# A fused attention and gated-FFN kernel: sums of x and weight sums move to other places and to another engine

## The chip, the cores and the metric

The kernel runs on one core of one Trainium2 chip. The metric is the time of one execution on the device in microseconds (us). The core has a matrix engine (TensorE; in the profile PE, and PEld for its weight loads), a vector engine (VectorE, DVE), a scalar engine (ScalarE, ACT), GpSimd (POOL), a queue engine that issues transfers here (SyncE, SP), and DMA engines that carry the transfers. Matmul results are written to PSUM, which is held here as four tiles of two banks each; everything else on the chip lies in SBUF.

## The reference, cut to what matters

A sigmoid attention of 8 sequences of 448 with 12 heads of 64 is followed by a gated feed-forward block on the 3584 x 768 result.

```python
def _attn_ref(q, k, v):                      # (8, 12, 448, 64) each
    scores = scale * np.matmul(q, k.transpose(0, 1, 3, 2)) - np.log(S)
    attn = 1.0 / (1.0 + np.exp(-scores))
    return np.matmul(attn, v)

def _moe_ref(x, w_gate, w_val, w_out):       # x (3584, 768), w_gate and w_val (768, 1536), w_out (1536, 768)
    g = x @ w_gate
    silu = g * (1.0 / (1.0 + np.exp(-g)))
    val = x @ w_val
    return silu * val @ w_out
```

## The kernel before

The 8 sequences are taken in four pairs (pb = 0 to 3). A quad is four heads of one sequence, so there are 24 quads, n = 0 to 23, three to a sequence (NJ = 3), and quad n belongs to sequence n // 3. Each quad has 7 attention tiles (C = 7). The attention of later sequences is laid between the feed-forward work of earlier ones as "visits" of three or four attention tiles.

For the first three pairs the first stage is ffn1 (12 units of 12 matmuls for each sequence) and the output stage is ffn2 and ffn2_group. The groups use Strassen-like sums: 7 block products in place of 8, for which sums of the hidden values h (make_sums, on VectorE) and of the output weights (w_sum, on VectorE) are needed. The last pair (FAST) does its first stage in the same way, in six steps of `double`: it needs sums of x (x_sums) and of the gate and value weights (fast_w).

The sums of the gate and value weights. There are 4 slices of them (s = 0 to 3). Slices 0 and 1 are made on GpSimd in pieces of 384 columns, three to a sum; slices 2 and 3 on VectorE in one piece each. The sums of kind 1 are written over the weights themselves:

```python
    def fast_w(s, kind, i=None):
    ... (b11, b12, b21, b22 are blocks of the gate and value weights, t is the output)
        a, b, op = {
            3: (b22, b12, SUB), 1: (b12, b11, SUB), 2: (b22, gT.get((s, 1), gT[(s, kind)])[:, js], SUB),
            4: (b21, gT.get((s, 2), gT[(s, kind)])[:, js], SUB),
        }[kind]
        (V if i is None else G).tensor_tensor(out=t, in0=a, in1=b, op=op)
```

The sums of x. They are formed when the last of the two sequences' quads of one index has left PSUM, so for quads 21, 22 and 23 (j = 0, 1, 2). The third is written over one of its operands:

```python
    def x_sums(pb, j):

        a11, a12 = xT[(2 * pb, 2 * j)], xT[(2 * pb, 2 * j + 1)]
        a21, a22 = xT[(2 * pb + 1, 2 * j)], xT[(2 * pb + 1, 2 * j + 1)]
        if j == 0:
            ts = [half_of(ramp_a)[:, 8 * FW * hw + i * S:8 * FW * hw + (i + 1) * S] for i in range(3)]
        else:
            ts = [xtp.tile([128, S], FP16, tag="xT", name=f"xS{i}_{pb}_{j}") for i in range(3)]
        s1, s2, s4 = ts
        V.tensor_tensor(out=s1, in0=a21, in1=a22, op=ADD)
        V.tensor_tensor(out=s2, in0=s1, in1=a11, op=SUB)
        V.tensor_tensor(out=a21, in0=a11, in1=a21, op=SUB)
        V.tensor_tensor(out=s4, in0=a12, in1=s2, op=SUB)
        xS[(pb, j)] = (s1, s2, a21, s4)
```

They are called at the end of pv, the product of attention and v, behind the casts that bring its result from PSUM to x:

```python
    ...
        x = xtp.tile([128, S], FP16, tag="xT", name=f"xT_{b}_{2 * j}")
        first = nc.vector.tensor_copy(out=x, in_=P[:, 0, :S])
        xT[(b, 2 * j)] = x
        x = xtp.tile([128, S], FP16, tag="xT", name=f"xT_{b}_{2 * j + 1}")
        xT[(b, 2 * j + 1)] = x
        halves = [(x[w * 64:(w + 1) * 64, :], P[(1 - w) * 64:(2 - w) * 64, 1, :S]) for w in range(2)]
        done = [nc.vector.tensor_copy(out=o, in_=i) for o, i in halves[how:]]
        if how == 2:
            for o, i in halves:
                apart(nc.scalar.copy(out=o, in_=i), first)
        sums = lambda: x_sums(b // 2, j) if b // 2 in FAST and b % 2 else None
        if how != 1:
            sums()

        def rest():
            if how == 1:
                o, i = halves[0]
                apart(nc.scalar.copy(out=o, in_=i), first, *done)
                sums()

        return rest
```

A double step uses the products in the order 1, 2, 6, 5, 7, 3, 4, each for two hidden blocks f; product 6 is the first that reads sums of x and of weights:

```python
        prods = {
            1: (w(wg16, 0), x(b0, 0)), 2: (w(wg16, 1), x(b0, 1)), 3: (w(wv16, 1), xs(4)), 4: (ws(4), x(b1, 1)),
            5: (ws(1), xs(1)), 6: (ws(2), xs(2)), 7: (ws(3), xs(3)),
        }
```

A group of the output stage. TensorE may write bank 0 again (product 6) when VectorE has taken product 1 out of it:

```python
        o1 = osp.tile([128, DM], FP32, tag="osb", name="osb")
        mm(1, 0, True, False)
        snap(0, o1, 0)
        mm(2, 1, True, True)
        put(1, o1, 0)
        ...
        mm(6, 0, False, False)
        snap(0, o1, 1)
        ... (products 5, 7, 3, 4 in the same way)
```

The order of the output stage's units, with the eight output weight sums of the first pair:

```python
        o_units = [(0.0, make_sums, (99,)), (FU2, ffn2, (pb, C - 1))]
        if pb == 0:

            ts = [(0.0, w_sum, (s, kind)) for s in range(2) for kind in (3, 2, 1, 4)]
            o_units += ts[:4] + [(FU2, ffn2, (pb, 0))] + ts[4:] + [(FU2, ffn2, (pb, 3))]
        for g in range(1 if pb == 0 else 0, 3):
            o_units.append((FU3, ffn2_group, (pb, g)))
        units += o_units
```

The attention's transfers. `fetch` issues the loads of a quad from GpSimd, `casts` turns q and k to bf16 on GpSimd, `trans` issues their DMA transposes from SyncE, and `hold` keeps GpSimd's queue until the transposes have landed, so that the loads behind it don't start sooner:

```python
    def fetch(n):
        load(n, 0, G)
        load(n, 1, G)
        load_v(n)
...
    def casts(n):
        cast(n, 0, G)
        cast(n, 1, G)

    def trans(n):
        trans_dma(n, 0)
        trans_dma(n, 1)

    def ready(n):
        casts(n)
        trans(n)

    held = one.tile([128, 2], BF16, tag="held", name="held")

    def hold(n):
        for w in range(2):
            G.tensor_copy(out=held[:, w:w + 1], in_=qT[(n, w, C - 1)][:, :1])
...
    plan = {
        (3, 2): ((casts, 5), (post.append, 4)),
        (3, 4): ((post.append, 5),),
        (4, 0): ((fetch, 6),),
        (4, 4): ((ready, 6),),
        (5, 4): ((hold, 6), (fetch, 7), (w_out, 0)),
        (6, 0): ((ready, 7),),
        (6, 4): ((hold, 7), (fetch, 8), (w_out, 1)),
        (7, 0): ((ready, 8),),
        (7, 4): ((hold, 8), (fetch, 9), (w_out, 2), (w_out, 3)),
        (8, 0): ((ready, 9),),
        (8, 4): ((hold, 9), (fetch, 10), (casts, 10)),
        (9, 0): ((trans, 10), (fetch, 11)),
    }
    for n in range(9, NQ):
        if n + 2 < NQ:
            plan[(n, 4)] = ((casts, n + 2),)
            plan[(n + 1, 0)] = ((trans, n + 2),)
        if n + 3 < NQ:
            plan[(n, 4)] += ((fetch, n + 3),)
```

A key (n, c) is done in the visit that holds attention tile c of quad n.

The loop that emits everything; its last lines place the weight sums of slices 0 and 1:

```python
    for at, (fn, args, how) in enumerate(seq):
        if fn is None:
            pvs, pend = pend, []
            attn_step(args, pvs, how)
            ... (the plan's actions)
        if pend and (... or fn is double or how):
            for n in pend:
                pv(n)
            pend = []
        fn(*args)
        if fn is ffn1 and args[0] == 2 * (B // 2 - 1) - 1 and args[1] == NF - 1:
            for sl in range(2):
                for kind in (3, 1, 2, 4):
                    for i in range(JT):
                        fast_w(sl, kind, i)
```

The order of emission around the third pair's output stage, as this code gives it: ffn1 of sequence 5 with the visits of quads 20 to 22; make_sums; ffn2(2, 6); visit of quad 23 with pv(22); ffn2_group(2, 0); visit of quad 23's last tiles; ffn2_group(2, 1); pv(23); ffn2_group(2, 2); the six double steps of the last pair. At quads 8 to 10, in the output stage of the first pair: visit (8, 0); two units of ffn1; visit (8, 4); ffn2(0, 6); four output weight sums; ffn2(0, 0); visit (9, 0) with pv(8); four output weight sums; ffn2(0, 3); visit (9, 4); ffn2_group(0, 1); visit (10, 0) with pv(9).

Of the kernel before, what the change touches and what calls it, by code (L numbers as in the profile page):

```python
# [14 lines left out]
ADD = mybir.AluOpType.add  # L15
SUB = mybir.AluOpType.subtract
# [4 lines left out]
def kernel(  # L21
# [13 lines left out]
    B, H, S, D = q.shape  # L35
    DM = H * D
    DFF = moe_w_gate.shape[1]
    C = S // D
    NJ = H // 4
    NP = H // 2  # L40
    NF = DFF // 128
# [101 lines left out]
    def half_of(a):  # L143
        return a.rearrange("p a b s -> p (a b s)").bitcast(FP16)
# [76 lines left out]
    def trans_pe(n):  # L221
        D2 = Banked()
        ds = [qkT.tile([128, C, 128], BF16, tag=f"T{w}", name=f"T{w}_{n}") for w in range(2)]
        for f in [trans_part(D2, w, n, w, 0, C, nc.vector, ds[w]) for w in range(2)]:
            f()
        qT[(n, 0)] = ds[0]
# [34 lines left out]
    def pv(n, how=0, at=None):  # L261
# [25 lines left out]
# [6 lines that stand above are left out]
# [10 lines left out]
    V, G = nc.vector, nc.gpsimd  # L303
# [44 lines left out]
    HF = NF // 2  # L348
    JT = NP // 2
# [3 lines left out]
    def fast_w(s, kind, i=None):  # L353

        js = slice(0, JT) if i is None else slice(i, i + 1)
        b11, b21 = wg16[s][:, 0::2][:, js], wg16[s][:, 1::2][:, js]
        b12, b22 = wv16[s][:, 0::2][:, js], wv16[s][:, 1::2][:, js]
        if (s, kind) not in gT:
            if kind == 1:
                gT[(s, 1)] = wv16[s][:, 0::2]  # L360
            else:
                at = s * 3 + (3, 2, 4).index(kind)
                a = half_of(stg_a) if at < 6 else pt_a.rearrange("p a b s -> p (a b s)")
                n = JT * FW * 128
                gT[(s, kind)] = a[:, at % 6 * n:(at % 6 + 1) * n].rearrange("p (j n) -> p j n", j=JT)
        t = gT[(s, kind)][:, js]
# [3 lines that stand above are left out]
        }[kind]  # L370
        (V if i is None else G).tensor_tensor(out=t, in0=a, in1=b, op=op)

    xS = {}

    def x_sums(pb, j):
# [5 lines that stand above are left out]
        else:  # L381
            ts = [xtp.tile([128, S], FP16, tag="xT", name=f"xS{i}_{pb}_{j}") for i in range(3)]
        s1, s2, s4 = ts
        V.tensor_tensor(out=s1, in0=a21, in1=a22, op=ADD)
        V.tensor_tensor(out=s2, in0=s1, in1=a11, op=SUB)
        V.tensor_tensor(out=a21, in0=a11, in1=a21, op=SUB)
        V.tensor_tensor(out=s4, in0=a12, in1=s2, op=SUB)
        xS[(pb, j)] = (s1, s2, a21, s4)

    def double(pb, fs, extra=()):  # L390
# [68 lines left out]
    hS = {}  # L459
# [161 lines left out]
    FU1, FU2, FU3, FU4 = 2.26, 3.9, 6.83, 7.85  # L621
# [3 lines left out]
    for pb in range(B // 2):  # L625
        if pb in FAST:
            late = [(s, kind) for s in (2, 3) for kind in (3, 1, 2, 4)]
            for f in range(0, NF, 2):
                extra = [lambda a=a: fast_w(*a) for a in (late[f:f + 2] if f < 8 else [])]
                units.append((FU4, double, (pb, (f, f + 1), extra)))  # L630
                tt += FU4
        for b in (2 * pb, 2 * pb + 1) if pb not in FAST else ():
            f1_start[b] = tt
            for f in range(NF):
                if b or f > 2:
                    units.append((FU1, ffn1, (b, f)))
                tt += FU1
            f1_end[b] = tt
        o_units = [(0.0, make_sums, (99,)), (FU2, ffn2, (pb, C - 1))]
        if pb == 0:  # L640

            ts = [(0.0, w_sum, (s, kind)) for s in range(2) for kind in (3, 2, 1, 4)]
            o_units += ts[:4] + [(FU2, ffn2, (pb, 0))] + ts[4:] + [(FU2, ffn2, (pb, 3))]
        for g in range(1 if pb == 0 else 0, 3):
            o_units.append((FU3, ffn2_group, (pb, g)))
        units += o_units
        tt += sum(u[0] for u in o_units)
# [8 lines left out]
    for grp in visits:  # L656
        n, c = grp[0]
        b, j = divmod(n, NJ)
# [6 lines left out]
    def attn_step(group, pvs, how):  # L665
        for part in (group[:2], group[2:]):
            scs = [(n, c, qk_tile(n, c)) for n, c in part]
            rest = [pv(pvs.pop(0), how) for _ in range(len(pvs))]
            for i, (n, c, sc) in enumerate(scs):

                sig_tile(n, c, sc, split=len(group) == 4 and part[0] == group[0] and i == 1)
            for f in rest:
                f()
# [50 lines left out]
    held = one.tile([128, 2], BF16, tag="held", name="held")  # L724
# [70 lines left out]
    for f, Df in enumerate(early):  # L795
# [14 lines left out]
        (6, 4): ((hold, 7), (fetch, 8), (w_out, 1)),  # L810
        (7, 0): ((ready, 8),),
        (7, 4): ((hold, 8), (fetch, 9), (w_out, 2), (w_out, 3)),
        (8, 0): ((ready, 9),),
        (8, 4): ((hold, 9), (fetch, 10), (casts, 10)),
        (9, 0): ((trans, 10), (fetch, 11)),
    }
    for n in range(9, NQ):
# [31 lines left out]
# [4 lines that stand above are left out]
            if at == last_visit:  # L853
                nc.scalar.preload_act_table(SILU)
            for n, c in args:
                for act, of in plan.get((n, c), ()):
                    act(of)
                if c == C - 1:
                    pend.append(n)
            while post:  # L860
                trans_pe(post.pop())
            continue
        if pend and (fn is ffn1 and args[1] == 0 and (args[0], NP - 1) not in xT or fn is double or how):
            for n in pend:
                pv(n)
            pend = []
        fn(*args)
        if fn is ffn1 and args[0] == 2 * (B // 2 - 1) - 1 and args[1] == NF - 1:
            for sl in range(2):
                for kind in (3, 1, 2, 4):  # L870
                    for i in range(JT):
                        fast_w(sl, kind, i)


# [28 lines left out]
```

## Time and profile before

| what | value |
|---|---|
| time, median of 3 executions | 414.78 us (414.24 to 425.22) |
| profiled execution, span from first to last instruction | 412.3 us |
| mean granted TensorE clock | 0.994 of full speed |
| busy: TensorE matmuls, VectorE, ScalarE, GpSimd | 96%, 65%, 52%, 29% of the span |
| 24 weight sums on GpSimd, 128 x 384 each | 22.3 us busy |
| sums of x on VectorE, 12 of 128 x 448 | 4.7 us busy |
| sums of h on VectorE, 96 of 128 x 384 | 39.1 us busy |

How to read the profile. Times are counted from the span's start. L311 is line 311 of the kernel. A line of the timeline gives the start, the duration, the engine, the line, the operation, output and inputs by the program's names with their shapes, how many, and in brackets the idle time before it with what ended it. A line of the list of waits says which instruction waited for which, with the total, the number and the longest. The chain of waits is followed back from the last instruction, at each step to what released it; its pieces have a start, a length and what it was. A busy TensorE need not be at its peak, because the ends of its pipelined matmuls are modelled.

### The profile page before, as it was taken

How to read it: one execution, taken by the hardware profiler on the slowest of the kernel's cores; microseconds unless marked ns; L12 is line 12 of the kernel's file. 1: busy time of each engine (PE TensorE's matmuls, PEld its weight loads, DVE VectorE, ACT ScalarE, POOL GpSimd, SP SyncE). 2: the span in 40 equal slices, each digit the busy share in tenths (PEclk: the TensorE clock that was granted, in tenths of full speed). 3: DMA queues.
4: the chain of work that ended last, by engine and by line, in shares of the span. 5: the costliest groups of instructions: out<-in, count | busy, mean ns of one | idle time of the engine just before them, and what ended most of it. 6: DMA issues, size and time to landing. Idle time of an engine off the chain costs nothing.

```text
span 412.3 us, 7991 instructions
## 1 busy us (share of the span) xinstructions
PE 397.2 (96%) x3158; PEld 206.3 (50%) x3158; DVE 269.6 (65%) x503; ACT 216.3 (52%) x332; POOL 119.1 (29%) x156
## 2 busy tenths in 40 slices
PE   7799999999989999999999999998998899999995
PEld 3445444545555454444555545444554455555563
DVE  3737565877944655587655556569966667996753
ACT  5966877554434666557454365755653226657100
POOL 4628051452535255330030333439400000000000
PEclk8999999999999999999999999999999999999999
DMA  8999968978899999751068797820002420000135
GB/s 267 248 255 244 228 135 127 199 162 155 249 202 320 171 193 191 194 131 13 13 129 232 181 164 134 148 45 2 1 2 67 126 78 1 2 1 0 40 81 148
DMA packets 59844, 54.38 MB, mean 132 GB/s; under 512 B 35744, under 2 KB 53280, under 8 KB 59808
## 3 DMA queue, kind: packets, MB, share of 16 engines
q0 software_dynamic: 18880, 30.94, 35.1%
q1 hardware_dynamic: 40496, 22.62, 26.5%
q8 instruction: 24, 0.39, 0.4%
q10 hardware_dynamic: 432, 0.33, 0.3%
q14 instruction: 12, 0.10, 0.1%
HBM read 47.19 MB, written 11.01 MB: 141 GB/s over the span
## 4 chain that ended last, share of the span: by engine, by line
PE 76%; DMA 15%; DVE 6%; POOL 1%; issue 1%; SPq 0%; ACT 0%; DVEq 0%; POOLq 0%
PE ps_D L311 32%; PE ps_D L542 16%; PE ps_D L409 12%; DMA T<-c 8%; PE ps_D L272 7%; PE ps_D L239 6%; PE ps_D L600 3%; DMA stg_a<-in_k_dram 2%; DMA v<-in_v_dram 2%; DMA stg_a<-in_q_dram 2%; DVE S L501 1%; DVE xT L286 1%; POOL c L190 1%; DMA st<-in_q_dram 1%; DVE xT L281 1%
## 5 line engine op out<-in xcount | busy, mean ns | idle before, releaser
L258 ACT ACTIVATE pt_a<-ps_D 128x896 f16<-128x896 f32 x148 | 127.2, 919 | 76.5 <-PE ps_D L239 74.1
L311 PE MATMUL ps_D<-xT,wg 128*128 128x448 f16 x432 | 95.2, 353 | 1.7 <-DVE xT L286 0.8
L311 PE MATMUL ps_D<-xT,wv 128*128 128x448 f16 x432 | 94.8, 353 | 0.0
L331 DVE TENSOR_TENSOR t<-ps_D,s 128x448 f16<-128x448 f32 x72 | 44.8, 622 | 52.3 <-ACT s L329 51.1
L190 POOL CAST c<-stg_a 128x896 bf16<-128x896 f32 x40 | 37.7, 949 | 105.6 <-DMA T<-c 45.1
L329 ACT ACTIVATE s<-ps_D 128x448 f16<-128x448 f32 x72 | 39.5, 549 | 54.2 <-PE ps_D L311 46.7
L311 PEld LDWEIGHTS <-wg 128*128 128x128 f16 x432 | 39.7, 98 | 46.3 <-issue 13.1
L311 PEld LDWEIGHTS <-wv 128*128 128x128 f16 x432 | 42.2, 98 | 39.5 <-issue 0.4
L335 DVE SCALAR_TENSOR_TENSOR hT<-ps_D,t 128x448 f16<-128x448 f32 x72 | 45.0, 625 | 7.5
L239 PE MATMUL ps_D<-T,T 64*64 64x448 bf16 x644 | 43.9, 357 | 2.8 <-DMA T<-c 1.1
L542 PE MATMUL ps_D<-ramp_a,S 128*128 128x384 f16 x198 | 34.0, 326 | 3.0 <-DVE osb L553 3.0
L272 PE MATMUL ps_D<-pt_a,v 64*64 64x448 f16 x672 | 35.9, 350 | 0.4 <-DMA v<-in_v_dram 0.4
L542 PEld LDWEIGHTS <-S 128*128 128x128 f16 x264 | 25.8, 98 | 20.4 <-issue 3.4
L553 DVE TENSOR_SCALAR osb<-ps_D 128x384 f32<-128x384 f32 x43 | 23.9, 557 | 18.3 <-PE ps_D L542 17.8
L281 DVE CAST xT<-ps_D 128x448 f16<-128x448 f32 x24 | 15.0, 623 | 22.7 <-PE ps_D L272 22.6
L419 ACT ACTIVATE snap<-ps_D 128x448 f32<-128x448 f32 x36 | 18.6, 542 | 20.9 <-issue 14.6
L239 PEld LDWEIGHTS <-T 64*64 64x64 bf16 x644 | 14.9, 106 | 25.0 <-issue 16.5
L559 DVE SCALAR_TENSOR_TENSOR osb<-ps_D,osb 128x384 f32<-128x384 f32 x33 | 18.4, 557 | 13.0 <-PE ps_D L542 12.8
L542 PEld LDWEIGHTS <-hT 128*128 128x128 f16 x198 | 18.7, 98 | 14.6 <-issue 2.9
L272 PEld LDWEIGHTS <-v 64*64 64x64 f16 x672 | 19.4, 107 | 13.3 <-DMA v<-in_v_dram 0.9
L286 DVE CAST xT<-ps_D 64x448 f16<-64x448 f32 x41 | 25.5, 621 | 0.7
L183 POOL DMA_DIRECT2D v<-in_v_dram x24 | 17.9, 746 | 22.9 <-PE ps_D L239 21.5
(82 smaller groups left out, 404.3 us busy)
## 6 DMA issues: line engine op xcount, KB each, us to landing
out_dram<-osb SPq DMA_DIRECT2D x52, 192.0 KB, 3.8
stg_a<-in_q_dram POOLq DMA_DIRECT2D x20, 448.0 KB, 4.2
stg_a<-in_k_dram POOLq DMA_DIRECT2D x20, 448.0 KB, 5.9
v<-in_v_dram POOLq DMA_DIRECT2D x24, 224.0 KB, 7.6
wg<-in_moe_w_gate_dram POOLq DMA_DIRECT2D x4, 576.0 KB, 12.3
wv<-in_moe_w_val_dram POOLq DMA_DIRECT2D x4, 576.0 KB, 12.6
wo<-in_moe_w_out_dram POOLq DMA_DIRECT2D x4, 576.0 KB, 8.8
ramp_a<-in_q_dram SPq DMA_DIRECT2D x2, 448.0 KB, 6.4
```

The lines of the kernel that those rows point to most:

```text
L190: eng.tensor_copy(out=t.rearrange("p c h d -> p h c d"), in_=st.rearrange("p h (c d) -> p h c d", c=C))
L239: nc.tensor.matmul(out=sc[w * 64:(w + 1) * 64, h2, :S], lhsT=kt[r, w * 64:(w + 1) * 64], rhs=qt[r, :, w * 64:(w + 1) * 64], start=True, st ...
L258: nc.scalar.activation(out=pt, in_=sc[:, :, :S], func=SIGM, bias=sbias, scale=qkscale)
L272: nc.tensor.matmul(out=P[g:g + 64, h2, :S], lhsT=vt[r, h2, c * D:(c + 1) * D], rhs=pt[r, h2, :], start=(c == 0), stop=(c == C - 1),)
L286: done = [nc.vector.tensor_copy(out=o, in_=i) for o, i in halves[how:]]
L311: nc.tensor.matmul(out=D.t[:, i, :S], lhsT=(wg16, wv16)[i][f // FW][:, pr, cs], rhs=xT[(b, pr)], start=(pr == 0), stop=(pr == NP - 1),),
L329: D.read(nc.scalar.activation(out=s16, in_=D.t[:, 0, :S], func=SIGM), 0)
L331: D.read(nc.vector.tensor_tensor(out=t1, in0=D.t[:, 0, :S], in1=s16, op=MULT), 0)
L335: nc.vector.scalar_tensor_tensor(out=hT[(b // 2, f)][:, b % 2, :], in0=D.t[:, 1, :S], scalar=hsc(b // 2), in1=t1, op0=MULT, op1=MULT),
L409: nc.tensor.matmul(out=D.t[:, bank, :S], lhsT=W(f, j), rhs=X(j), start=(start and j == 0), stop=(stop and j == JT - 1), skip_group_check=True,
L542: nc.tensor.matmul(out=D.t[:, bank, :hw], lhsT=l, rhs=B_(i), start=(first and i == 0), stop=(i == HF - 1), skip_group_check=True,),
L553: nc.vector.tensor_scalar(out=o, in0=D.t[:, bank, :hw], scalar1=1.0 / hsc(pb), scalar2=None, op0=MULT), bank
```

## The change

Four things are moved.

1. The weight sums of slices 0 and 1 (`early_w`, still on GpSimd) are emitted inside the output stage of the third pair: slice 0 behind ffn2(2, 6), slice 1 behind ffn2_group(2, 0). Ahead of the first a copy of one column of the last sum of h keeps GpSimd's queue until VectorE has made it.
2. The sums of x of quads 22 and 23 (j = 1 and 2) go from VectorE to GpSimd. They are meant to leave VectorE free for the evictions behind them.
3. The last of the eight output weight sums comes one place later, behind ffn2(0, 3).
4. The load of quad 10 is issued right behind the casts of quad 9, and not in the next visit behind a wait for quad 9's transposes.

```diff
--- before.py
+++ after.py
@@ -370,6 +370,11 @@
         }[kind]
         (V if i is None else G).tensor_tensor(out=t, in0=a, in1=b, op=op)
 
+    def early_w(s):
+        for kind in (3, 1, 2, 4):
+            for i in range(JT):
+                fast_w(s, kind, i)
+
     xS = {}
 
     def x_sums(pb, j):
@@ -381,10 +386,11 @@
         else:
             ts = [xtp.tile([128, S], FP16, tag="xT", name=f"xS{i}_{pb}_{j}") for i in range(3)]
         s1, s2, s4 = ts
-        V.tensor_tensor(out=s1, in0=a21, in1=a22, op=ADD)
-        V.tensor_tensor(out=s2, in0=s1, in1=a11, op=SUB)
-        V.tensor_tensor(out=a21, in0=a11, in1=a21, op=SUB)
-        V.tensor_tensor(out=s4, in0=a12, in1=s2, op=SUB)
+        eng = G if j else V
+        eng.tensor_tensor(out=s1, in0=a21, in1=a22, op=ADD)
+        eng.tensor_tensor(out=s2, in0=s1, in1=a11, op=SUB)
+        eng.tensor_tensor(out=a21, in0=a11, in1=a21, op=SUB)
+        eng.tensor_tensor(out=s4, in0=a12, in1=s2, op=SUB)
         xS[(pb, j)] = (s1, s2, a21, s4)
 
     def double(pb, fs, extra=()):
@@ -640,7 +646,7 @@
         if pb == 0:
 
             ts = [(0.0, w_sum, (s, kind)) for s in range(2) for kind in (3, 2, 1, 4)]
-            o_units += ts[:4] + [(FU2, ffn2, (pb, 0))] + ts[4:] + [(FU2, ffn2, (pb, 3))]
+            o_units += ts[:4] + [(FU2, ffn2, (pb, 0))] + ts[4:7] + [(FU2, ffn2, (pb, 3))] + ts[7:]
         for g in range(1 if pb == 0 else 0, 3):
             o_units.append((FU3, ffn2_group, (pb, g)))
         units += o_units
@@ -810,8 +816,8 @@
         (6, 4): ((hold, 7), (fetch, 8), (w_out, 1)),
         (7, 0): ((ready, 8),),
         (7, 4): ((hold, 8), (fetch, 9), (w_out, 2), (w_out, 3)),
-        (8, 0): ((ready, 9),),
-        (8, 4): ((hold, 9), (fetch, 10), (casts, 10)),
+        (8, 0): ((ready, 9), (fetch, 10)),
+        (8, 4): ((casts, 10),),
         (9, 0): ((trans, 10), (fetch, 11)),
     }
     for n in range(9, NQ):
@@ -865,11 +871,11 @@
                 pv(n)
             pend = []
         fn(*args)
-        if fn is ffn1 and args[0] == 2 * (B // 2 - 1) - 1 and args[1] == NF - 1:
-            for sl in range(2):
-                for kind in (3, 1, 2, 4):
-                    for i in range(JT):
-                        fast_w(sl, kind, i)
+        if fn is ffn2 and args == (B // 2 - 2, C - 1):
+            G.tensor_copy(out=held[:, :1], in_=hS[(args[0], 4, HF - 1)][:, :1])
+            early_w(0)
+        if fn is ffn2_group and args == (B // 2 - 2, 0):
+            early_w(1)
 
 
 # ---- launch: one core; inputs and outputs as the reference has them ----
```

## The prediction

> **What bounds the kernel now.** I read the page's shares first, then the waits of TensorE, then the chain of waits, then the timelines of VectorE and GpSimd around each wait. The shares say that TensorE is the bound:
>
> ```profile
> PE 397.2 (96%) x3158; PEld 206.3 (50%) x3158; DVE 269.6 (65%) x503; ACT 216.3 (52%) x332; POOL 119.1 (29%) x156
> ```
>
> So the change, which takes no matmul away, can only win back TensorE's idle time: 412.3 - 397.2 = 15.1 us in the whole span, some 5 us of it the start and the tail. The waits of TensorE name the rest:
>
> ```profile
> PE ps_D L542 <- DVE osb L553: 3.0, 2, 1.9
> ...
> PE ps_D L239 <- DMA T<-c: 1.1, 1, 1.1
> ...
> PE ps_D L311 <- DVE xT L286: 0.8, 1, 0.8
> PE ps_D L311 <- DVE t L331: 0.7, 1, 0.7
> ```
>
> (us in total, times, longest.) These four lines, 5.6 us, are the ones that the change touches. I take them one at a time.
>
> *The first line* is the output stage of the third pair. The chain there, start and length:
>
> ```profile
> 309.93 0.63 DVE xT L286
> 310.65 0.40 DVE xS L384
> 311.08 0.39 DVE xS L385
> 311.47 0.10 DVE xT L386
> 311.57 0.12 issue
> 311.69 0.38 DVE xS L387
> 312.07 0.48 DVE osb L553
> 312.59 5.04 PE ps_D L542 x30
> ```
>
> The sums of x (L384 to L387) stand in VectorE's queue between the casts of x and the first eviction L553. TensorE needs that eviction before it may write the bank again. The same happens with quad 23: casts to 328.73, sums from 328.77 to 330.18, eviction to 330.66, TensorE on at 330.71.
>
> *The last two lines* are the end of the first stage of the third pair, where GpSimd forms the weight sums. VectorE and GpSimd in that stretch and VectorE after it (start, length):
>
> ```profile
> 276.81 2.77 POOL L371 TENSOR_TENSOR stg_a<-wv 128x384 f16<-128x384 f16 x3
> 279.54 2.88 POOL L371 TENSOR_TENSOR stg_a<-wg,stg_a 128x384 f16<-128x384 f16 x3
> ```
>
> ```profile
> 279.83 0.95 DVE L501 TENSOR_TENSOR S<-S,hT 128x384 f16<-128x384 f16 x1
> ...
> 282.62 0.62 DVE L331 TENSOR_TENSOR t<-ps_D,s 128x448 f16<-128x448 f32 x1
> ...
> 300.40 0.36 DVE L501 TENSOR_TENSOR S<-S,hT 128x384 f16<-128x384 f16 x1
> ```
>
> The same sum of two fp16 SBUF tiles takes 0.95 us while GpSimd adds and 0.36 us when GpSimd is idle. The operation L331, which reads a PSUM operand, takes its usual 0.62 us.
>
> *The second line* is quad 10's transpose, which the chain shows as
>
> ```profile
> 107.34 3.01 DMA stg_a<-in_q_dram
> 110.35 10.57 DMA T<-c
> ```
>
> with TensorE free at 119.83 and on at 120.97.
>
> [...] 0.95 against 0.36 us for the sums, and 0.62 us unmoved for operations with one operand in PSUM. [...] I scale GpSimd's additions with their columns. [...] the pair of transposes of quad 6 lands 3.4 and 3.9 us after issue, that of quad 10, with loads and stores beside it, 11.4 and 10.6 us.
>
> **The change part by part.**
>
> *1. Weight sums moved behind the h sums.* Before, 24 GpSimd additions run from 274.2 to 293.7 beside the h sums. After, a one-column copy on GpSimd reads the last h sum, so they start when VectorE has done it. What they cost TensorE now can be read from a twin: the first stage of the second pair (130.85 to 200.90) has the same 288 + 140 matmuls of L311 and L272 and the same visits, but no additions on GpSimd. It takes 70.05 us, and the third pair's (231.50 to 303.28) takes 71.78. The difference, **1.73 us**, is what this part should give back. The gaps agree: units of 12 matmuls that start 2.27 us apart elsewhere start 3.23 us apart at 279.41 (0.96 more), and three attention tiles that take 0.69 us elsewhere take 1.51 at 287.27 (0.82 more), 1.78 together.
>
> *2. Sums of x of quads 22 and 23 on GpSimd.* With them out of VectorE's queue, the eviction follows the casts. Quad 22: casts end at 310.55, eviction to 311.15, while TensorE has its own work to 309.44 + 12 x 0.1625 = 311.39. So TensorE does not wait; before, it went on at 312.59. Gain about **1.2 us**. Quad 23 has three casts on VectorE, to 328.73. The eviction then ends at 329.30 and not at 330.66, and TensorE, done at 328.60, still waits some 0.7 us. Gain **1.36 us**. The lengths of the groups say the same: 6.92 us for the undisturbed one (318.28 to 325.20), 8.12 for the one behind quad 22, 8.93 for the one behind quad 23.
>
> *Does GpSimd come in time?* Its queue after the change is: 12 weight sums (first slice), 4 sums of x (quad 22), 12 weight sums (second slice), 4 sums of x (quad 23). Three undisturbed additions take 2.65 us, 0.88 each at 384 columns, so an estimate of 0.88 x 448 / 384 = 1.03 us at 448. The last h sum ends at 305.53, so about 303.8 after part 1. From there 12 x 0.88 = 10.6 to 314.4; 4.1 to 318.5; 10.6 to 329.1; 4.1 to 333.2. The last stage begins at 335.58 - 1.73 - 2.56 = 331.3. Its third product, 2.27 us later, reads the second of quad 23's sums at about 333.9; GpSimd has that one at 329.1 + 2.06 = 331.2, 2.7 us ahead. The fourth sum, at 333.2, is read at about 337. The second slice's weights are read from the second double step on, at 339 or later. So nothing waits, and VectorE's own 2-operand additions of that stage begin only as GpSimd ends.
>
> *3. The eighth output weight sum, one place later.* It takes 0.75 us at 111.34 on VectorE, ahead of an eviction that starts at 112.15, when TensorE has just finished (112.14). After, it falls between that eviction (to 113.17) and the next (114.02): 113.17 + 0.75 = 113.92. Gain and loss: **0**, unless a GpSimd cast runs beside it and stretches it to some 1.5 us, as one was at 105.04.
>
> *4. Quad 10's load not held.* Before, GpSimd waits until 99.9 for quad 9's transposes, loads quad 10 from 100.36 and casts it to 107.4. After, the load is issued at 91 us, right behind quad 9's casts. Quad 10's transpose does not start sooner by that: on its queue it stands behind stores that wait for an eviction at 107.46, and it went out at 108.71. What changes is its company. Before, quad 11's loads (from 107.34) run beside it. After, they can be issued from about 103, and what is beside it is their end and quad 12's loads from about 111. I expect the transpose to land 0.5 to 1.5 us sooner and credit half of the wait of 1.14: **0.5 us**.
>
> Sum: 1.73 + 1.2 + 1.36 + 0.5 = 4.8 us. 414.78 - 4.8 = **410.0 us**, 1.2% less.
>
> **The rivals.**
>
> *GpSimd is late.* If its additions took 1.03 us each, as the slowest do beside VectorE (12 x 1.03 = 12.4, and 1.2 for a sum of x), quad 23's second sum would come at 303.8 + 12.4 + 4.8 + 12.4 + 2.4 = 335.8, and TensorE would wait 2 us: about 412. Against it: after the last h sum VectorE has only evictions and casts from PSUM until the last stage, and those disturb nothing in this trace (a cast of x at 281.33 beside GpSimd still takes 0.63).
>
> *The contention goes along with the work.* If the evictions (two fp32 operands, one in PSUM) suffered as the h sums do, each would take about 1 us and TensorE, which needs one per 0.98 us, would lose up to 5 us: about 415. Against it: an eviction at 124.42 beside a GpSimd cast takes 0.56 as elsewhere, and L331, which has one operand in each memory as the second kind of eviction has, was unmoved beside GpSimd's additions.
>
> *Quad 10's load collides with quad 9's transposes.* Those are issued at 89.44 and 91.02 beside the last output weights and land at 98.9 and 99.8; TensorE needs them at 105.93. Even the longest landing of the trace, 11.4 us, gives 102.4. I expect no wait; if the output weights, needed from about 99.5 and landing by 98.4, were pushed back instead, TensorE would lose 1 to 3 us and the time would be 411 to 413. They are in the same queue ahead of the new load, which speaks against it.
>
> *The gain of quad 10 is all or nothing.* All of it gives 409.4; none, because quad 12's loads take the place of quad 11's, 410.5.
>
> **Range and chances.** Parts 1 and 2 rest on measured gaps that the change removes by order alone, 4.3 us with perhaps 0.3 of error. Part 4 is between +1.1 and -2. So 80% from 408.9 to 412.2. Over 2% (below 406.5) would need more than all that the touched waits hold: 0.03. Slower by over 2% would need a new wait of 13 us: 0.02. Within 2%: 0.95.
>
> **What would show it.** Right: h sums of the third pair at 0.36 us throughout and its first stage at 70.0 us; the waits on evictions from 3.0 to about 0.7 us, once; the last stage some 4.5 us earlier; GpSimd's last sum done within 2 us of its start. Wrong: a wait of the double step's matmuls on GpSimd's sums; evictions of 1 us; a wait for quad 9's transposes or for the output weights near 99 to 106; quad 10's wait still 1 us or longer.

## The result, and the profile after

| | before | after |
|---|---|---|
| time, median | 414.93 us | 411.40 us |
| ratio, 95% interval | | 0.9917 (0.9892 to 0.9941) |
| span of the profiled execution | 412.3 us | 410.0 us |
| predicted | | 410.0 us (408.9 to 412.2) |

The change makes the kernel 0.8% faster, between 0.6% and 1.1%, some 3.4 us of the 4.8 us predicted. The ratios here leave out executions more than 1.5% above their kernel's fastest, so a median of all executions can lie above what its ratio says.

The shares of the page after the change:

```profile
PE 397.2 (97%) x3158; PEld 206.3 (50%) x3158; DVE 263.7 (64%) x495; ACT 216.4 (53%) x332; POOL 125.6 (31%) x163
```

TensorE's busy time is the same 397.2 us; only the idle time around it became less. VectorE's busy time fell by 5.9 us: it has 8 sums of x less to make, and its sums of h are no longer stretched: ten of those of the third pair took 0.48 to 1.06 us before, and none takes more than 0.36 us after. The waits of TensorE after (total, times, longest, us):

```profile
PE ps_D L239 <- DMA T<-c: 1.7, 1, 1.7
...
PE ps_D L548 <- DVE osb L559: 0.6, 1, 0.6
PE ps_D L606 <- DMA wo<-in_moe_w_out_dram: 0.5, 1, 0.5
PE ps_D L239 <- DVE xT L286: 0.4, 1, 0.4
PE ps_D L548 <- DVE osb L619: 0.4, 1, 0.4
```

(L548, L559, L606 and L619 are L542, L553, L600 and L613 of before, and L507 below is L501.) The waits on the evictions of the third pair are down from 3.0 to 0.6 us, and those of L311 are gone. But there is a transpose wait again, of 1.7 us and not 1.1, and two waits that were not there before: on the last output weights and on an eviction L619.

The chain behind quad 23, where the sums of x stood between casts and eviction:

```profile
327.06 0.62 DVE xT L286
327.68 0.03 issue
327.71 0.57 DVE osb L559
328.28 0.04 issue
328.32 5.04 PE ps_D L548 x30
```

The eviction now follows the cast at once. VectorE's timeline in the stretch where GpSimd used to add:

```profile
280.18 0.35 DVE L507 TENSOR_TENSOR S<-hT,hT 128x384 f16<-128x384 f16 x1
280.56 0.36 DVE L507 TENSOR_TENSOR S<-S,hT 128x384 f16<-128x384 f16 x1
```

The h sums take 0.36 us there, as the prediction asked, and not 0.95. GpSimd in the output stage of the third pair:

```profile
305.74 0.19 POOL L875 CAST held<-S 128x1 bf16<-128x1 f16 x1 [43.55 <-DVE S L507]
305.89 2.65 POOL L371 TENSOR_TENSOR stg_a<-wv 128x384 f16<-128x384 f16 x3
...
316.32 1.03 POOL L390 TENSOR_TENSOR xS<-xT,xT 128x448 f16<-128x448 f16 x1
...
331.94 1.03 POOL L391 TENSOR_TENSOR xS<-xS,xT 128x448 f16<-128x448 f16 x1
```

The copy holds the queue until the last h sum is made, three weight sums take 2.65 us and a sum of x 1.03 us, which is what the prediction scaled. An eviction L559 at 318.40, beside these additions, takes the usual 0.56 us.

The start of the first matmul of each stage, from TensorE's timeline, gives the length of each stage (us). The first column is the output stage of the first pair, the second the first stage of the second pair, then the first and the output stage of the third pair, and the six double steps. The second pair's output stage took 30.62 or 30.63 us in every run and is left out.

| kernel | output 1 | first 2 | first 3 | output 3 | double |
|---|---|---|---|---|---|
| before | 32.80 | 70.02 | 71.76 | 32.35 | 47.78 |
| after | 32.68 | 71.82 | 70.01 | 29.82 | 47.79 |
| whole change, again | 32.04 | 70.02 | 70.01 | 29.82 | 47.79 |
| parts 1 and 2 | 33.25 | 72.65 | 70.01 | 29.82 | 47.79 |
| part 1 | 32.81 | 70.01 | 70.01 | 34.56 | 47.78 |
| part 2 | 32.49 | 70.02 | 71.75 | 29.82 | 47.78 |
| part 4 | 32.74 | 70.02 | 71.76 | 32.35 | 48.11 |
| without part 3 | 39.72 | 70.02 | 70.01 | 29.82 | 47.79 |
| six weight sums more | 32.45 | 70.70 | 70.02 | 29.82 | 52.04 |
| change, split cast | 33.42 | 70.01 | 70.01 | 29.21 | 47.79 |
| change, holds, split cast | 32.18 | 70.02 | 70.01 | 29.21 | 47.78 |
| parts 1 and 2, holds (11, 13 to 17), split cast | 31.59 | 75.28 | 70.01 | 29.21 | 47.79 |
| change, holds, split cast, early weights | 37.21 | 70.01 | 70.01 | 29.21 | 47.97 |
| parts 1 and 2, holds (13 to 17), split cast | 32.14 | 70.01 | 70.01 | 29.21 | 47.79 |

Two halves can be read from it. The three columns on the right follow the code to a few hundredths of a microsecond, but for two entries under double: 48.11 (part 4), where TensorE waits 0.28 us for VectorE at 366.5 us, and 47.97 (early weights). Why VectorE is late there is open. The two on the left do not follow the code: "before", "parts 1 and 2", "part 1" and "part 2" have the same instructions up to 230 us, and still differ by up to 0.8 us in the first and by 2.6 us in the second. The first profile after the change is one of those with a long second column, 1.8 us over the usual 70.02.

### The profile page after: what moved, and what is told of

Read it like the earlier page. It is cut to its first block, busy times and chain, and to the rows that moved or that the text cites. A ratio compares the mean times of both kernels' runs of the same rounds, so it can differ in the third digit from the quotient of the medians.

```text
span 410.0 us, 7992 instructions
## 1 busy us (share of the span) xinstructions
PE 397.2 (97%) x3158; PEld 206.3 (50%) x3158; DVE 263.7 (64%) x495; ACT 216.4 (53%) x332; POOL 125.6 (31%) x163
## 4 chain that ended last, share of the span: by engine, by line
PE 68%; DMA 22%; POOL 5%; DVE 2%; SPq 2%; issue 1%; POOLq 0%; DVEq 0%
PE ps_D L311 24%; PE ps_D L548 18%; PE ps_D L415 12%; DMA stg_a<-in_k_dram 10%; DMA T<-c 7%; PE ps_D L239 5%; PE ps_D L272 5%; PE ps_D L606 4%; DMA wo<-in_moe_w_out_dram 3%; DMA ramp_a<-in_q_dram 2%; POOL c L190 1%; POOL stg_a L178 1%; SPq L518 1%; POOL wv L133 1%; DVE ramp_a L476 1%
## 5 line engine op out<-in xcount | busy, mean ns | idle before, releaser
L311 PE MATMUL ps_D<-xT,wg 128*128 128x448 f16 x432 | 95.3, 353 | 0.1
L311 PE MATMUL ps_D<-xT,wv 128*128 128x448 f16 x432 | 94.8, 352 | 0.0
L311 PEld LDWEIGHTS <-wg 128*128 128x128 f16 x432 | 39.7, 98 | 44.6 <-issue 11.3
L311 PEld LDWEIGHTS <-wv 128*128 128x128 f16 x432 | 42.2, 98 | 39.5 <-issue 0.4
L559 DVE TENSOR_SCALAR osb<-ps_D 128x384 f32<-128x384 f32 x43 | 24.0, 557 | 17.6 <-PE ps_D L548 16.8
L548 PEld LDWEIGHTS <-S 128*128 128x128 f16 x264 | 25.8, 98 | 17.8 <-issue 0.8
L548 PE MATMUL ps_D<-ramp_a,S 128*128 128x384 f16 x198 | 34.0, 326 | 0.6 <-DVE osb L559 0.6
L565 DVE SCALAR_TENSOR_TENSOR osb<-ps_D,osb 128x384 f32<-128x384 f32 x33 | 18.4, 558 | 13.2 <-PE ps_D L548 13.1
L548 PEld LDWEIGHTS <-hT 128*128 128x128 f16 x198 | 18.8, 98 | 15.0 <-issue 3.2
L606 PE MATMUL ps_D<-wo,hT 128*128 128x384 f16 x144 | 24.4, 326 | 0.5 <-DMA wo<-in_moe_w_out_dram 0.5
## 6 DMA issues: line engine op xcount, KB each, us to landing
wg<-in_moe_w_gate_dram POOLq DMA_DIRECT2D x4, 576.0 KB, 11.9
```

Source lines behind the costliest of these rows:

```text
L311: nc.tensor.matmul(out=D.t[:, i, :S], lhsT=(wg16, wv16)[i][f // FW][:, pr, cs], rhs=xT[(b, pr)], start=(pr == 0), stop=(pr == NP - 1),),
L548: nc.tensor.matmul(out=D.t[:, bank, :hw], lhsT=l, rhs=B_(i), start=(first and i == 0), stop=(i == HF - 1), skip_group_check=True,),
L606: nc.tensor.matmul(out=D.t[:, half, :hw], lhsT=h[:, m * 128:(m + 1) * 128], rhs=wo16[f // FW][:, f % FW, half * hw:(half + 1) * hw], start ...
```

## The experiments

Theory A, from the first comparison of the two traces: parts 1 and 2 give the predicted 4.3 us, and part 4 takes about one back through new collisions of transfers. Theory B: part 4 is neutral, as nearly predicted. The first four runs take the change apart.

**Parts 1 and 2 alone.** The edit against the whole change puts the loads and the output weight sums back:

```diff
-            o_units += ts[:4] + [(FU2, ffn2, (pb, 0))] + ts[4:7] + [(FU2, ffn2, (pb, 3))] + ts[7:]
+            o_units += ts[:4] + [(FU2, ffn2, (pb, 0))] + ts[4:] + [(FU2, ffn2, (pb, 3))]
-        (8, 0): ((ready, 9), (fetch, 10)),
-        (8, 4): ((casts, 10),),
+        (8, 0): ((ready, 9),),
+        (8, 4): ((hold, 9), (fetch, 10), (casts, 10)),
```

> Parts 1 and 2 alone (weight sums behind the h sums, sums of x of quads 22 and 23 on GpSimd), loads and output weight sums as before. Theory A (the two parts give the 4.3 us of the prediction, and part 4 of the change took 0.8 to 1.7 us of it back): span 408 us, time about 410.6, faster than the whole change; TensorE waits for quad 10's transpose as before (1.1 us), not for quad 12's, not for the output weights. Theory B (part 4 is neutral and the missing microsecond is chance of the loads): time as the whole change, 411.4, with a wait for some transpose after 140 us here too.

Measured: 410.75 us, ratio 0.9922 (0.9899 to 0.9946). The median is what theory A expected, but the ratio is not apart from the whole change's 0.9917, and the profile is much as theory B had it (a wait for some transpose after 140 us). It shows a wait of 2.57 us for quad 11's transpose at 139 us, in a kernel in which quad 10's load is held, and 0.42 us for quad 10's, where A expected 1.1 again:

```profile
122.08 0.57 PE L239 MATMUL ps_D<-T,T 64*64 64x448 bf16 x8 [0.42 <-DMA T<-c]
...
139.20 0.57 PE L239 MATMUL ps_D<-T,T 64*64 64x448 bf16 x8 [2.57 <-DMA T<-c]
```

The kernel before has the same instructions up to there and waits for quad 10 only. So such waits are no mark of part 4. The saving by the ratio is 3.2 us (2.2 to 4.2); the 4.3 us of theory A lie just outside, though the medians, 414.99 and 410.75, are 4.24 us apart.

**Part 4 alone.**

```diff
-        (8, 0): ((ready, 9),),
-        (8, 4): ((hold, 9), (fetch, 10), (casts, 10)),
+        (8, 0): ((ready, 9), (fetch, 10)),
+        (8, 4): ((casts, 10),),
```

> Part 4 alone (quad 10's load right behind quad 9's casts). Theory A: the wait for quad 10's transpose (1.1 us) goes, but the last output weights land at about 100 us (wait 0.5 to 0.7), VectorE's output weight sums meet GpSimd's casts and hold an eviction (0.4 to 1.2), and quad 12's transposes land late (wait 1.7): 416 to 417, 1 to 2 us slower than before. Theory B (as predicted): 0.5 us faster, 414.4, with no new wait.

Measured: 415.85 us, ratio 1.0018 (0.9994 to 1.0042): between 0.25 us faster and 1.7 us slower. B's gain of 0.5 us lies outside; of A's loss of 1 to 2 us the intervals exclude only the upper end. But none of the three new waits that A named is in the profile: TensorE waits neither for the output weights nor for the eviction behind their sums nor for quad 12. The wait that part 4 was to remove is there:

```profile
120.81 0.57 PE L239 MATMUL ps_D<-T,T 64*64 64x448 bf16 x8 [1.08 <-DMA T<-c]
```

**Part 1 alone.** The edit of parts 1 and 2, and the sums of x stay on VectorE, in effect:

```diff
-        eng = G if j else V
+        eng = V
```

> Part 1 alone: weight sums behind the h sums, sums of x on VectorE. Theory A (contention moves with the additions): the first stage of the third pair takes 70.0 us and gives 1.7 back, but quad 22's four sums of x, now beside GpSimd's additions, take about 1.1 us each in place of 0.39, which holds the eviction some 2.8 us longer: 415 to 416, no faster than before. Theory B (the parts add up): 413.2.

Measured: 416.56 us, ratio 1.003 (1.0005 to 1.0056), slower. The first stage of the third pair gives its 1.75 us (71.76 to 70.01), and the output stage takes 2.21 us more (32.35 to 34.56). The timeline of VectorE behind quad 22's casts shows where:

```profile
309.56 0.59 DVE L389 TENSOR_TENSOR xS<-xT,xT 128x448 f16<-128x448 f16 x1
310.18 0.98 DVE L390 TENSOR_TENSOR xS<-xS,xT 128x448 f16<-128x448 f16 x1
311.09 1.09 DVE L391 TENSOR_TENSOR xT<-xT,xT 128x448 f16<-128x448 f16 x1
312.10 1.09 DVE L392 TENSOR_TENSOR xS<-xT,xS 128x448 f16<-128x448 f16 x1
313.12 0.54 DVE L558 TENSOR_SCALAR osb<-ps_D 128x384 f32<-128x384 f32 x1
```

From the first sum to the eviction it is 3.56 us, against 1.34 before (310.65 to 311.99): 2.22 us, the loss of the stage. The eviction itself, which reads PSUM, takes 0.54 us beside the same additions. Theory A was right here in kind; its 2.8 us were too much because the first of the four was barely touched (0.59). Behind quad 23, where GpSimd was done, the sums take 0.39 us again. The two stages together lose 2.21 - 1.75 = 0.46 us, 0.1%; that lies inside the interval, and what the rest of the measured 0.3% is stays open.

**Part 2 alone.** The edit of parts 1 and 2, and the weight sums stay where they were, right behind the last ffn1:

```diff
-        if fn is ffn2 and args == (B // 2 - 2, C - 1):
-            G.tensor_copy(out=held[:, :1], in_=hS[(args[0], 4, HF - 1)][:, :1])
-            early_w(0)
-        if fn is ffn2_group and args == (B // 2 - 2, 0):
-            early_w(1)
+        if fn is ffn1 and args[0] == 2 * (B // 2 - 1) - 1 and args[1] == NF - 1:
+            ... (the 24 weight sums, as before)
```

> Part 2 alone: sums of x of quads 22 and 23 on GpSimd, weight sums where they were. Both theories: the waits on evictions fall from 3.0 to about 0.6 us and the output stage of the third pair is 2.5 us shorter, the first stage stays at 71.8 us: 412.4. If it gains less, GpSimd's sums come late for the last stage.

Measured: 412.06 us, ratio 0.9941 (0.9914 to 0.9969); output stage 29.82 us, 2.53 less than before, first stage 71.75. As expected. So part 1 has no value of its own: alone its two stages lose 0.46 us, and on top of part 2 its stage gives 1.75 us. The whole times, 412.06 and 410.75 us, point the same way, with intervals that overlap.

These runs bring theory C: between 85 and 150 us loads, stores and transposes share the DMA engines with little to spare (in the page of before every slice of 10 us there has them 70% busy or more), what lands late differs from execution to execution, and part 4 is worth nothing that can be measured.

**The whole change, again.** No edit.

> The whole change once more, beside the others on one chip. Theory A (part 4 costs about 1 us net): 411.4 to 412, slower than parts 1 and 2 alone. Theory C (what happens between 85 and 150 us, where loads, stores and transposes share the DMA engines, differs from execution to execution, and part 4 is worth nothing that can be measured): within 0.5 us of parts 1 and 2 alone, and the wait for a quad's transposes sits in another place in this profile than in the first one.

Measured: 410.68 us, ratio 0.9886 (0.9841 to 0.9930), six executions from 408.85 to 416.20. Theory C expected the wait for a transpose in another place; in this profile TensorE waits for no transpose and for no output weights at all. Of the waits behind 30 us two are left:

```profile
PE ps_D L548 <- DVE osb L559: 0.6, 1, 0.6
...
PE ps_D L548 <- DVE osb L619: 0.4, 1, 0.4
```

The span is 407.8 us, with the same code as the first profile's 410.0. So the 1.7 us and the 0.5 us of the first profile do not belong to every execution of the changed kernel. The chip is no rival for this scatter: parts 1 and 2, part 1 and part 2 ran on one chip with the same instructions up to 230 us, and their first stages of the second pair are 72.65, 70.01 and 70.02 us.

What part 4 does do, in every profile, is to delay quad 9's transposes: issued between 86.8 and 93.9 us, they land 12.9 to 16.3 us later in the seven profiles that have part 4 and the weights' loads in their place, and 8.0 to 11.0 us later in the six that hold quad 10's load. For quad 10's transposes no such split is seen: 4.6 to 11.9 us with part 4, 3.9 to 11.4 us without it (3.4 to 4.6 where quad 11's load is held as well).

**Without part 3.** The whole change with the eighth output weight sum back in its place:

```diff
-            o_units += ts[:4] + [(FU2, ffn2, (pb, 0))] + ts[4:7] + [(FU2, ffn2, (pb, 3))] + ts[7:]
+            o_units += ts[:4] + [(FU2, ffn2, (pb, 0))] + ts[4:] + [(FU2, ffn2, (pb, 3))]
```

> The whole change with the eighth output weight sum back ahead of the eviction. As predicted (part 3 is worth 0): same time and stage times as the whole change. Theory D (GpSimd's casts stretch the output weight sums, and the eviction behind four of them holds TensorE): the wait on that eviction at about 113 us grows from 0.4 to between 0.8 and 1.5 us, time 0.5 to 1 us above the whole change.

Measured: median of seven 416.33 us, four of them from 416.33 to 419.11 and three at 410.2 or 410.3; ratio 0.9874 (0.9819 to 0.9929), against 0.9886 for the whole change on the same chip. The profile is one of the long executions (416.93), and its output stage of the first pair takes 39.72 us:

```profile
101.74 8.18 PE L606 MATMUL ps_D<-wo,hT 128*128 128x384 f16 x39 [1.98 <-DMA wo<-in_moe_w_out_dram]
...
126.35 0.57 PE L239 MATMUL ps_D<-T,T 64*64 64x448 bf16 x8 [2.17 <-DMA T<-c]
```

The output weights landed at 101.7 us, before the moved sum comes up at all, and quad 10's transposes at 126.3; behind each wait the granted clock is 0.50 for 3.4 us, so that the 39 matmuls behind the first take 8.18 us, and not 6.50 as in the whole change's first profile. Neither wait is on the eviction that theory D means. That one is 0.37 us (0.39 in the whole change's first profile), so the growth to between 0.8 and 1.5 us did not come.

The wait on that eviction follows the time that the output weight sums ahead of it take, from the first one's start to the last one's end. Part 4 alone has four in 2.9 us and no wait; without part 3 there are four in 3.5 us and a wait of 0.37; in parts 1 and 2 four in 4.2 us, two of them stretched to 1.37 and 1.48 beside casts on GpSimd, and 0.64; in the whole change three in 3.6 us, two of them stretched in the same way (1.37 and 1.48 us, where 0.75 us is usual), and 0.39. Where the casts fall beside the sums, part 3 may thus save some 0.25 us (an estimate, 0.64 - 0.39). Nothing of that size can be shown in the times.

**Six weight sums more.** How much time GpSimd has to spare for the last stage: the second slice's first sum is made three times.

```diff
-        for kind in (3, 1, 2, 4):
+        for kind in ((3, 1, 2, 4) if s == 0 else (3, 3, 3, 1, 2, 4)):
```

> The whole change with six additions more on GpSimd: the second slice's first sum is made three times over, so 6 x 0.88 = 5.3 us lie ahead of quad 23's sums of x. Theory (GpSimd's sums have slack and are not on the path): in the changed kernel the second sum of quad 23 ends at 332.97 and TensorE reads it at about 335.84, 2.9 us later; six more use that up, and TensorE waits some 2.4 us in the last stage's first step: that stage goes from 47.79 to about 50.2 us, all other stages stay. Rival (there is no slack, the last stage already waits for it unseen): 5 us longer. Rival (TensorE doesn't depend on it there): no change.

Measured: 415.10 us, ratio 0.9987 (0.9960 to 1.0015). The waits name what the prediction had as its first rival:

```profile
PE ps_D L415 <- POOL xS L391: 2.6, 1, 2.6
```

The wait is 2.6 us where 2.4 was expected, so the slack of about 2.9 us is real, and TensorE does hang on the second sum of quad 23. (That sum itself takes 1.42 us here and not 1.03, beside weight sums that VectorE has begun.) But the stage grew by 4.25 us, almost the 5 us of the rival without slack; the time alone would have misled. The view by stretches of time (TensorE's busy time is the second entry, its granted clock the entry behind POOL's) shows the rest:

```profile
336.00:337.00 1.00, 0.07 (x1) 0.07 (x1) 0.97 (x1) 0.00 (x0) 1.00 (x2) 0.77 0.01 0
337.00:338.00 1.00, 1.00 (x3) 0.33 (x3) 0.49 (x1) 0.50 (x1) 1.00 (x1) 0.50 0.00 0
338.00:339.00 1.00, 1.00 (x4) 0.44 (x3) 0.00 (x0) 0.42 (x2) 1.00 (x2) 0.50 0.04 8
339.00:340.00 1.00, 1.00 (x4) 0.42 (x3) 0.00 (x0) 1.00 (x4) 0.38 (x1) 0.52 0.00 0
340.00:341.00 1.00, 1.00 (x7) 0.51 (x6) 0.00 (x0) 0.98 (x3) 0.00 (x0) 1.00 0.00 0
```

After the wait TensorE runs at half its clock until 340 us: 10 matmuls from 336.93 to 340.30 take 3.37 us, where 10 x 0.189 = 1.89 us is usual, 1.48 us more. With the gap itself, from 334.15, where the next matmul was due, to 336.93, that makes 2.78 + 1.48 = 4.26 us, the growth of the stage.

**A better version: split cast and holds.** Two things were left in the profile after: 0.6 us for quad 23's eviction, which stands behind three casts, and the waits for transposes. The first edit gives one of the casts to ScalarE, which the kernel already does for quad 22; the second holds the loads of quads 13 to 17 until the transposes ahead of them have landed:

```diff
             for n in pend:
-                pv(n)
+                pv(n, 1 if fn is ffn2_group else 0)()
...
-            plan[(n, 4)] += ((fetch, n + 3),)
+            plan[(n, 4)] += (((hold, n + 1),) if 10 <= n <= 14 else ()) + ((fetch, n + 3),)
```

With the whole change:

> The whole change, with the loads of quads 13 to 17 held until the transposes before them have landed, and one of quad 23's casts on ScalarE. Theory C: no wait for the transposes of quads 10 to 15, only the 0.7 us for the last output weights and some 0.4 us for an eviction are left: 409 to 409.8. Theory A: the output weights' wait stays 0.5 to 0.7 us and quad 9's transposes land after 105 us, so this is 0.5 us slower than the version that holds quad 10's load.

Measured: 409.98 us, ratio 0.9868 (0.9837 to 0.9899), all six executions between 409.36 and 410.57. The output stage of the third pair is 29.21 us, 0.61 less, and no transpose is waited for. The wait of 0.7 us for the last output weights, expected on both theories, is not there either; they landed at 100.4 us.

With the split cast alone (the first half of the edit):

> The whole change with one of quad 23's casts on ScalarE and no holds. Output stage of the third pair 29.21 us as in the versions with both. Theory C: the median lies 0.6 us under the whole change, about 410, and the times scatter over several us as the whole change's do. If they scatter as little as those of the version with holds (409.4 to 410.6), the holds do nothing.

Measured: median of six 412.44 us, ratio 0.9890 (0.9826 to 0.9955), executions from 408.37 to 415.58 us, again 29.21 us for the stage, and a wait for quad 10's transposes in this profile, with part 4 in place:

```profile
121.60 0.57 PE L239 MATMUL ps_D<-T,T 64*64 64x448 bf16 x8 [1.75 <-DMA T<-c]
```

The fastest executions are as fast as with the holds, the median is not. That the holds take the scatter away is what the two sets of six suggest; so few don't prove it, and the three versions with holds that follow scatter more (by 3.7 to 9.2 us).

With the loads of the output weights one visit earlier on top of both:

```diff
-        (5, 4): ((hold, 6), (fetch, 7), (w_out, 0)),
-        (6, 4): ((hold, 7), (fetch, 8), (w_out, 1)),
-        (7, 4): ((hold, 8), (fetch, 9), (w_out, 2), (w_out, 3)),
+        (5, 4): ((hold, 6), (fetch, 7), (w_out, 0), (w_out, 1)),
+        (6, 4): ((hold, 7), (fetch, 8), (w_out, 2)),
+        (7, 4): ((hold, 8), (fetch, 9), (w_out, 3)),
```

> The whole change with the holds of quads 13 to 17, the split cast, and the output weights' loads one visit earlier each (weights 0 and 1 with quad 7, 2 with quad 8, 3 with quad 9). Theory: 0.56 MB less lies in front of quad 10's load and beside quad 9's transposes, so quad 9's transposes land before 103 us, TensorE doesn't wait for the last output weights, and what is left of the first output stage is at most 0.4 us: 409.2 to 409.8. Rival: the weights now collide with quad 7's and 8's transposes and TensorE waits there, before 90 us: 410 to 412.

Measured: 414.55 us, ratio 0.9972 (0.9946 to 0.9998): most of the gain is gone. No output weights are waited for, but quad 9's transposes are:

```profile
109.99 0.57 PE L239 MATMUL ps_D<-T,T 64*64 64x448 bf16 x8 [3.79 <-DMA T<-c]
```

Quad 7's transposes, beside two weights' loads, take 11.0 and 9.3 us to land (6.4 and 7.0 in the version without this edit), so the hold lets quad 8's load out at 74.3 us and not at 72.0, quad 9's at 88.7 and not at 85.1, and quad 9's second transpose goes out at 96.4 and not at 92.1. There it meets quad 10's load, issued from 96.3 on by part 4, and takes 13.6 us; the first one, issued at 93.6, takes 6.8. The rival was right that the loads collide with quad 7's transposes; the bill came two quads later, through the holds. A wait for quad 9's transposes beside quad 10's load is also what the prediction had among its rivals.

With parts 1 and 2 only, and quad 11's load held too:

```diff
-        (9, 0): ((trans, 10), (fetch, 11)),
+        (9, 0): ((trans, 10), (hold, 10), (fetch, 11)),
```

> Parts 1 and 2, without 3 and 4, and two things more: GpSimd holds the loads of quads 11 and 13 to 17 until the transposes before them have landed, and one of quad 23's three casts of x goes to ScalarE. Theory C: no wait for a transpose is left between 85 and 180 us in the profile, and the times scatter less: 408.5 to 409.5. The output stage of the third pair falls from 29.82 to 29.2 us, as the eviction comes 0.63 us sooner. Rival: held loads come late themselves and TensorE waits for casts and transposes further on, over 411.

Measured: 411.69 us, ratio 0.9898 (0.9854 to 0.9941), executions from 408.65 to 416.19, so no less scatter. Quad 10's transposes land in 3.4 to 4.6 us, but TensorE then waits 3.74 us for quad 11's at 138 us. Quad 11's load waits until 115.2, quad 12's follows at 121.2 and runs beside quad 11's transposes (issued at 121.9 and 123.4), which take 13.7 and 14.5 us. The rival was right: the hold moved the collision one quad on.

With parts 1 and 2, the holds of quads 13 to 17 and the split cast, without that hold and without parts 3 and 4:

> Parts 1 and 2, the holds of quads 13 to 17 and the split cast, without parts 3 and 4. Theory C (part 4 is worth nothing that can be measured): the time of the version with parts 3 and 4 and the same two additions, 410.0, within 0.6 us; quad 9's transposes land 8 to 11 us after their issue and not 13 to 16; output stage of the third pair 29.21 us. Theory A (part 4 costs a microsecond): 409. Rival (part 4 does give its half microsecond or more): 410.6 to 411.2.

Measured: 409.69 us, ratio 0.9884 (0.9843 to 0.9925); quad 9's transposes land in 8.5 to 9.2 us, and no transpose is waited for. That is the time of the version with parts 3 and 4, within 0.3 us, as theory C had it, but the two intervals would hide a microsecond either way. Both versions beat the kernel after the change by their medians, 411.4 or 410.7 against 410.0 and 409.7; their ratios overlap with its own.

## Why the prediction was right, and where it was not

- **Part 1, 1.73 us.** Right: the stage went from 71.76 to 70.01, 1.75 us, in every kernel that has the part. The twin stage of another pair was a good measure of what contention cost. What the step left out is that the part is worth this only together with part 2. Alone it cost 2.21 us in the next stage, because the sums of x are as open to GpSimd's additions as the h sums are (0.98 to 1.09 us against 0.39; the h sums up to 1.06 against 0.36).
- **Part 2, 1.2 and 1.36 us.** Right: 2.53 us for the sum of 2.56. TensorE goes on behind quad 22 without a wait, and behind quad 23 after 0.6 us (0.7 predicted).
- **GpSimd in time.** Right: 2.65 us for three additions and 1.03 for one of 448 columns. Six additions more showed the slack, some 2.9 us where the prediction worked out 2.7.
- **Evictions and casts untouched by GpSimd.** Right: 0.56 us for an eviction and 0.62 us for a cast of x (at 309.42) beside its additions, as elsewhere.
- **Part 3, 0.** Nothing else could be shown in the times. The rider, that a cast may stretch the sum, fell on the sums ahead of the eviction in both profiles of the whole change and came with a wait of 0.4 us.
- **Part 4, 0.5 us.** This step failed. It credited half of a wait of 1.14 us that one profile showed, and expected quad 10's transpose to land sooner in other company. But that wait is a matter of the execution: it was 0.4 us in the profile of parts 1 and 2 and absent in those of part 1 and part 2, all with the same instructions up to there, and 1.08 us with part 4 alone. The time from issue to landing shows no gain either (4.6 to 11.9 us with part 4, 3.9 to 11.4 without). Alone, part 4 changes the time by between -0.06% and +0.42%, so a gain of 0.5 us (0.12%) lies outside; beside the other parts the runs are too few to tell.
- **"Even the longest landing of the trace, 11.4 us, gives 102.4".** Wrong: with a load more beside them quad 9's transposes took up to 16.3 us and landed at 105.6 and 106.3, and TensorE got to them at 106.78. The largest figure of a trace is no bound for a heavier load.
- **"They are in the same queue ahead of the new load, which speaks against it".** Left open. In the first profile the last output weights landed at 100.3 and not at 98.4, and TensorE waited 0.5 us; in the second profile it did not. But part 2 alone, without the new load, had them at 99.9 and a wait of 0.35 us, so the wait is no mark of part 4. From issue to landing they took 11.8 to 13.1 us in the seven profiles with the new load and 10.8 to 12.7 us in the six without: later by perhaps a microsecond, with ranges that overlap.

The sum of the steps that hold, 1.75 + 2.53 = 4.28 us, is 1.0% and lies inside both intervals of the change (0.6 to 1.1% and 0.7 to 1.6%). The first measurement, 0.8%, came out under it, and its profiled execution shows 1.7 us for quad 12's transposes that the second doesn't have. For parts 1 and 2 alone the interval (0.5 to 1.0%) ends just short of it: its profile shows 3.0 us of waits for transposes, which the stages on the right of the table do not. That the measured 411.4 and 410.7 lie near the predicted 410.0 is no support for part 4.

## What to carry to other kernels

Work that was moved away from a contended stretch took its contention along (in part 1 alone three sums of x took 0.98 to 1.09 us in place of 0.39): look what the other engine does at the new place, and move that first. A stage that has a twin elsewhere in the trace, with the same matmuls and without the suspect, gave the cost of the suspect to a few hundredths of a microsecond (1.73 predicted, 1.75 measured). Where the DMA engines were 70% busy or more, as between 85 and 150 us here, a wait of a microsecond in one profile was often that execution's alone; before crediting its removal, compare two profiles of kernels with the same instructions up to there.

## What the runs showed that was not expected

- A wait of TensorE can cost more than its length, and its length alone does not say when. In each case below where the clock fell, the half clock lasted 3.41 us. In the traces of before, after and without part 3 two such stretches start a whole multiple of 3.413 us apart: at 8.05 and 410.82 us before (118 times), at 8.31 and 407.67 after (117 times), at 102.94 and 126.84 without part 3 (seven times). On that reading each trace is cut here into intervals of that length, and the idle time of TensorE is counted in each. Two figures in a row stand for the two intervals that the wait falls into:

| kernel | wait | idle in the interval | clock in the interval after |
|---|---|---|---|
| parts 1 and 2 | 2.57 us | 0.89 and 1.68 us | 1.00 and 1.00 |
| part 1, quad 22 | 3.25 us | 1.99 and 1.25 us | 1.00 and 1.00 |
| without part 3, weights | 1.98 us | 1.98 us | 0.50 |
| without part 3, quad 10 | 2.17 us | 2.17 us | 0.50 |
| six weight sums more | 2.62 us | 2.24 and 0.39 us | 0.50 and 1.00 |
| early weights | 3.79 us | 1.50 and 2.29 us | 1.00 and 0.50 |
| parts 1 and 2, holds (11, 13 to 17) | 3.74 us | 3.32 and 0.42 us | 0.50 and 1.00 |

The wait of 3.25 us is cut in two by a boundary at 312.46 (from 309.05 to there TensorE is busy with matmuls for 1.42 of 3.41 us) and costs nothing more; one of 1.98 us that falls into one interval does. In these traces the clock fell where about 2.0 us or more of one interval were idle; 1.98 and 1.99 us, on the two sides, are too near to each other to be told apart, since the ends of matmuls are modelled, so no exact limit is shown.
- Four kernels with the same first 230 us differed by up to 2.6 us in one stage of it, while the second pair's output stage repeated to 0.01 us in every run.
